# One PSUM tile per bank for the second mix, the attention product and the last part; attention in two blocks of work; an engine's own releases ahead of its pick

## The chip, the cores and the metric

The kernel runs on one core of a Trainium2 chip. The metric is device time in microseconds (us) of one execution; the median of three runs of the kernel before is 1122.73 us (1122.41 to 1123.28). A traced execution of it took 1125.21 us, with a span of 1123.4 us from its first to its last instruction; all rows below come from that execution.

## The reference

Attention with mixed heads (4 batches, 12 heads, 448 positions, 64 channels per head, all in 32-bit floats) is followed by two feed-forward layers over the 1792 rows that it makes:

```
scores = scale * matmul(q, k^T)                      # per batch and head
scores = einsum('bhij,hg->bgij', scores, w_pre)      # first mix, over heads
attn   = softmax(scores)
attn   = einsum('bhij,hg->bgij', attn, w_post)       # second mix, over heads
x      = matmul(attn, v)                             # attention product
h1 = ((x @ w1) * (x @ w2)) @ w3;   x1 = h1 @ w_out   # 768 -> 1024 -> 1024 -> 768
h2 = max(x1 @ m1, x1 @ m2, x1 @ m3); out = h2 @ m_out
```

The program fuses w3 and w_out into one matrix, and does every dense product with three passes over numbers that are split in a high and a low part.

## The kernel before

The program has two parts. The first is a list of pieces of work that `Plan` collects and orders; the second (`last_two`, from `seven`) is written in plain order and the framework schedules it.

In the first part the attention of all four batches runs, and beside it the fusing of weights (line 658) and the dense layers of batches 0 and 1 (line 753) fill TensorE (PE in the rows). A step of attention takes up to 20 query rows. Its PE pieces are: scores (line 379, tile `s`; in the beginning also `m` and `p`), the first mix (line 446, into `m`), and one step later the second mix (line 485, into `p`). ScalarE (ACT) and VectorE (DVE) reduce, take the exponential and evict. The evictions of the second mix go into the tile `a`: two copies by `copy` at line 280, one for each bank of `p`. After six steps (five or six in the last group of a batch) `attend` multiplies `a` by `v`: 36 matmuls over 128 rows (line 519) and then 12 over two halves of 64 rows for the last 64 keys (line 529), all into the two banks of `p`. Both banks are then evicted, for batch 0 into `X` (a copy by ACT and a subtraction by DVE each, line 541), otherwise into `xs`, and go to DRAM.

What stands in which order is set by `Plan.order`: it plays the pieces through with a cost for each (the second argument of `plan`), and an engine that comes free takes the ready piece with the smallest key; PE adds 0.5 (`STAY`) to the key of a piece in another mode. Modes are `q` (scores and both mixes, tiles of 64 rows), `a` (attention product) and `d` (dense and fusing, 128x128). In the event loop the end of a piece first makes the engine free (kind 0), then the engine picks, and only then are the pieces released that wait for the ended one on the same engine (kind 3); other engines' pieces follow after 0.12 (kind 1). So a dense piece that continues the one just ended is not yet on the list when PE picks.

All PSUM tiles come from one pool. `m`, `p` and `s` are tiles of two banks each (`banks`), and two single banks `w` serve the dense products: eight banks in all. The last part does the layers of batches 2 and 3 with seven products of half size instead of eight (`seven`); its accumulators p1 and p2 are the two banks of `m`, p6 and p5 those of `p`, p7 and p3 those of `s`, and p4 a `w` bank. ACT or DVE read each accumulator while PE goes on with the next (lines 997 to 1023), with weights that ACT and DVE split (lines 816 and 817).

Of the kernel before, what the change touches and what calls it, by code (L numbers as in the profile page):

```python
# [69 lines left out]
class Plan:  # L70
# [21 lines left out]
    def order(self):  # L92
# [25 lines left out]
        while True:  # L118
# [62 lines left out]
def attention_talking_heads_moe_kernel(  # L181
# [23 lines left out]
    stages = ctx.enter_context(ExitStack())  # L205
    pa = stages.enter_context(tc.tile_pool(name="pa", bufs=2))

    sdram = [dram.tile([S, H, S], F32, name=f"sdram_{b}") for b in range(B)]
# [4 lines left out]
    def bank():  # L213
        return ps.tile([P, 512], F32, tag="w", name="w", bufs=2)

    def banks(tag):
        return ps.tile([P, 2, 512], F32, tag=tag, name=tag, bufs=1)

# [112 lines left out]

    pm, pp, pz = (banks(x) for x in "mps")
    pw = [bank() for _ in range(2)]
# [30 lines left out]
    later = []  # L364

    def unit(b, r, u, slot, key, room="s"):

        whole = P * (r + 1) <= S
        parts = [(u, 0), (u, HB)] if whole else [(2 * u, 0), (2 * u + 1, 0)]
        pt = {"m": pm, "p": pp, "s": pz}[room]  # L370

# [3 lines left out]
        def multiply(_):  # L375
            for c, (pr, i) in enumerate(parts):
                for o in range(2):
                    sl = slice(o * D, (o + 1) * D)
                    nc.tensor.matmul(  # L379
                        pt[HB * c:HB * c + HB, o, :S], q[sl, pr, i:i + HB], kall[sl, pr], start=True, stop=True  # L380
                    )
# [3 lines left out]
        if r == 0 and b == 0:  # L385
            out, where = at[:, 2 * S * u:2 * S * (u + 1)], ("arow", u)
            out = out.rearrange("p (o j) -> p o j", o=2)
        else:
            n = turn("s", 2)
            out, where = st[n], ("st", n)  # L390

        def evict(e):
            if e == "ACT":
                nc.scalar.activation(out, pt[:, :, :S], AF.Copy, scale=D ** -0.5)
            else:
                nc.vector.tensor_scalar_mul(out, pt[:, :, :S], D ** -0.5)  # L396

        plan({"ACT": 0.95, "DVE": 1.12}, 0, key + 0.05, evict, bank_of, [where])
        if whole:
            x = 0 if r or b else P - 80  # L400
            reads = [where] if r or b else [("arow", y) for y in range(HP)]
            later.append(lambda: dma(
# [4 lines left out]
        else:  # L407
            for c, (pr, _) in enumerate(parts):
                dma("SP", key + 0.06, sdram[b][P * r:S, 2 * pr:2 * pr + 2], out[HB * c:HB * c + HB], 229e3,
                    [where], [("sd", b, r, pr)])  # L410

    def regroup(b, p, key):
# [5 lines left out]
        if b == 0 and i < FIRST:  # L418
            row = at
            for c in range(2):  # L420
                for u in range(2):
                    z = ROW[(i + GI * c + GB * u) // GB]
                    dma("POOL", key, x[HB * u:HB * u + MR, c], row[z:z + WAYS * (GB - 1) + 1:WAYS], 108e3,
                        [("arow", pr) for pr in range(HP)], [("x", n, u, c)])
        elif i + 2 * GI <= S:
# [43 lines left out]
    def post(b, p, e2, key):  # L469
        c0, i0, w = chunk(p)  # L470
        e_, kwr = es[e2], kwrs[e2]
        a = at[:, :JR * w].rearrange("p (r i) -> p r i", i=w)
        pt = pp[:, :, :JR * GI].rearrange("p c (r x) -> p c r x", x=GI)
        halves = [c for c in range(2) if blocks_of(p)[c][0]]

        def multiply(_):
            for u in range(2):
                for t in range(JF + 1):
                    for side in range(2):
                        j, g = (P * t + HB * side, 0) if t < JF else (S - HB, HP * side)  # L480
                        n = H if t < JF else HP
                        for c in halves:
                            m = blocks_of(p)[c][u]
                            sl = slice(HB * c, HB * c + MR)
                            nc.tensor.matmul(  # L485
                                pt[HB * side:HB * side + HB, c, H * t:H * t + n, u * GB:u * GB + m],
                                e_[sl, u, j:j + HB], kwr[sl, u, g:g + n, :m], start=True, stop=True,
# [4 lines left out]
        for c in halves:  # L492
            n = sum(blocks_of(p)[c])
            off = 2 * GI * p - i0 + GI * c
            whole = [("a", y, z) for y in range(CP) for z in range(2)]
            rows = [("arow", u) for u in range(HP)] if p == 0 and b == 0 else []
            plan({"ACT": 0.52, "DVE": 0.61}, 0, key + 0.03, lambda e, c=c, n=n, off=off: copy(
                e, a[:, :, off:off + n], pt[:, c, :, :n]),
                [("p", c)], (whole if p % CP == 0 and c == 0 else [("a", p % CP, c)]) + rows)
# [8 lines left out]
    def attend(b, p, key):  # L508
        _, i0, n = chunk(p)
        a = at[:, :JR * n].rearrange("p (r i) -> p r i", i=n)  # L510
        pt = pp[:, :, :3 * n].rearrange("p b (x i) -> p b x i", x=3)
        whole = [("a", y, z) for y in range(CP) for z in range(2)]

        def multiply(_):
            for pr in range(HP):
                for t in range(JF):
                    for o in range(2):
                        h = 2 * pr + o
                        nc.tensor.matmul(  # L519
                            pt[o * D:(o + 1) * D, pr // 3, pr % 3], vt[:, t, h * D:(h + 1) * D], a[:, t * H + h],  # L520
                            start=(pr % 3 == t == 0), stop=False,
                        )
            for pr in range(3):
                for x in range(2):
                    sl = slice(HB * x, HB * x + HB)
                    for o in range(2):
                        g = 2 * pr + o
                        h = HP * x + g
                        nc.tensor.matmul(  # L529
                            pt[o * D:(o + 1) * D, x, pr], vt[sl, JF, h * D:(h + 1) * D], a[sl, JF * H + g],  # L530
                            start=False, stop=(pr == 2),
                        )

        plan("PE", 4.35 * n / (CG * GI), key, multiply, whole + [("v", 0), ("v", 1, 0), ("v", 1, 1)],
             [("p", 0), ("p", 1)], mode="a")
        for x in range(2):
            if b == 0:
                sl, i = slice(3 * x, 3 * x + 3), slice(i0, i0 + n)
                plan("ACT", 0.5, key + 0.05, lambda _, sl=sl, i=i, x=x: nc.scalar.copy(
                    rows("X")[0][:, sl, i], pt[:, x]), [("p", x)], [("Xh", x, p // CP)] + [("Xh", y) for y in range(3)] * (p // CP == 0))  # L540
                plan("DVE", 0.58, key + 0.06, lambda _, sl=sl, i=i, x=x: nc.vector.tensor_sub(  # L541
                    rows("X")[1][:, sl, i], pt[:, x], rows("X")[0][:, sl, i].bitcast(F32)),
                    [("p", x), ("Xh", x, p // CP)],
# [4 lines left out]
            plan({"ACT": 0.5, "DVE": 0.58}, 0, key + 0.05, lambda e, t=t, x=x: copy(  # L548
                e, t, pp[:, x, :3 * n]), [("p", x)], [("xs", k)])
            dma("SP", key + 0.06, xdram[b][3 * x:3 * x + 3, :, i0:i0 + n].rearrange("x p i -> p x i"),  # L550
# [268 lines left out]
    def tail_parts(pool_users, at_):  # L819
# [294 lines left out]
    def attention_parts():  # L1114
# [19 lines left out]
        while later:  # L1134
            later.pop(0)()
        slots[0, 1] = load_q(0, 1, -5.6, after=[("arow", 2)])
        yield -1.0
        en = {}
        for s in range(LAST + LAG):
            if s == 1:  # L1140
                load_v(0, 3.0, [("arow", 5), ("sd", 0, 1, 1)])
            for d in (s + 2,):
# [112 lines left out]
```

## Time and profile before

| | us |
|---|---|
| median of three runs | 1122.73 |
| profiled execution | 1125.21 |
| its span | 1123.4 |
| PE busy (97% of the span) | 1085.8 |
| weight loads on PE (79%) | 882.1 |
| DVE busy (69%) | 774.6 |
| ACT busy (51%) | 568.2 |
| DMA moved 258.79 MB | 230 GB/s mean |

PE is busy in nearly the whole span, so the question at each place is not who waits for PE but what PE loses between pieces. A matmul's shown duration overlaps with the next one's; what a run of matmuls takes is read from the start of its first one to the start of the next run. The busy time of PE hides such losses, and a bracket at a row's end shows idle time only where nothing at all ran.

### The profile page before, as it was taken

The page shows a single profiled execution, that of the slowest core. Times are in us where ns is not written, and L with a number is a line of the kernel's source. Part 1 is how long each engine was busy: PE and PEld are TensorE (multiplying, and loading weights), DVE is VectorE, ACT ScalarE, POOL GpSimd, SP SyncE. Part 2 cuts the span into 40 slices and gives each one's busy share as a digit, 9 for nine tenths or more (in the row PEclk, how much of TensorE's full clock was granted, in tenths as well). Part 3 has the DMA queues.
Part 4 walks back from the last instruction along what each step waited for, and adds up shares of the span by engine and source line. Part 5 has one row for each costly group of instructions (what it writes and reads, how often), then busy time and mean ns, then how long its engine had stood idle before and what let it go on. Part 6 is the DMA issues. An engine that isn't in the chain of part 4 may idle for free.

```text
span 1123.4 us, 29327 instructions
## 1 busy us (share of the span) xinstructions
PE 1085.8 (97%) x12348; PEld 882.1 (79%) x12348; DVE 774.6 (69%) x1374; ACT 568.2 (51%) x1119; POOL 84.2 (7%) x159
## 2 busy tenths in 40 slices
PE   5799999999999999999999999999999999999998
PEld 1477787777777878777776888889788899888877
DVE  4775676678766877667667677783877753687874
ACT  4775566666466667555445454353433343233331
POOL 5310010000000100000111111110000000000000
PEclk8699999999999999999999999999999999999999
DMA  8989898989886989898998899877333321333333
GB/s 248 346 277 314 249 308 277 311 305 309 269 281 195 323 289 307 285 312 278 288 313 286 269 296 322 267 237 263 116 99 109 113 63 47 92 99 106 113 115 117
DMA packets 109365, 258.79 MB, mean 230 GB/s; under 512 B 21342, under 2 KB 61858, under 8 KB 109234
## 3 DMA queue, kind: packets, MB, share of 16 engines
q1 hardware_dynamic: 90290, 172.61, 47.8%
q0 software_dynamic: 16928, 80.64, 21.9%
q10 hardware_dynamic: 2016, 3.67, 0.9%
q8 instruction: 97, 1.59, 0.6%
q14 instruction: 34, 0.28, 0.1%
HBM read 173.84 MB, written 81.74 MB: 227 GB/s over the span
## 4 chain that ended last, share of the span: by engine, by line
PE 88%; DVE 6%; DMA 4%; ACT 1%; issue 1%; DVEq 0%; SPq 0%; ACTq 0%
PE w L753 31%; PE w L224 8%; PE p L485 7%; PE p L224 6%; PE m L446 6%; PE w L658 6%; PE s L379 6%; PE m L224 5%; PE s L224 5%; PE p L519 5%; PE p L529 1%; DMA wlo<-kept_m 1%; DMA sdram<-s 1%; DMA q<-in_qT 1%; DMA vlo<-sums_o 1%
## 5 line engine op out<-in xcount | busy, mean ns | idle before, releaser
L485 PEld LDWEIGHTS p<-kwr,e 60*64 60x64 f32 x5760 | 103.6, 137 | 46.0 <-issue 27.7
L450 DVE TENSOR_REDUCE nmax<-m 128x2 f32<-128x896 f32 (+1 forms) x92 | 100.1, 1088 | 43.6 <-PE m L446 43.2
L453 ACT ACTIVATE e<-m,nmax 128x448 f32<-128x448 f32 (+1 forms) x184 | 115.5, 637 | 16.1 <-DVE nmax L450 15.6
L485 PE MATMUL p<-kwr,e 60*64 60x60 f32 (+1 forms) x5760 | 103.6, 219 | 4.5 <-DVE xs L280 2.0
L280 ACT COPY a<-p 128x420 f32<-128x420 f32 (+1 forms) x114 | 56.0, 524 | 100.8 <-PE p L485 93.6
L446 PE MATMUL m<-x,kp 60*64 60x448 f32 x720 | 89.8, 558 | 1.0 <-ACT e L453 0.9
L379 PE MATMUL s<-kall,q 64*64 64x448 f32 x640 | 80.1, 571 | 8.9 <-DVE s L396 5.6
L753 PE MATMUL w<-yhi,whi 128*128 128x448 f32 x216 | 82.1, 380 | 0.0
L753 PE MATMUL w<-yhi,wlo 128*128 128x448 f32 x216 | 79.1, 366 | 0.1
L753 PE MATMUL w<-ylo,whi 128*128 128x448 f32 x216 | 78.9, 365 | 0.0
L753 PE MATMUL w<-xhi,whi 128*128 128x448 f32 x192 | 73.4, 382 | 0.0
L753 PE MATMUL w<-xlo,whi 128*128 128x448 f32 x192 | 70.2, 366 | 0.9 <-DVE xlo L541 0.9
L753 PE MATMUL w<-xhi,wlo 128*128 128x448 f32 x192 | 70.2, 366 | 0.0
L816 ACT CAST whi<-wlo 128x768 fp32r<-128x768 f32 x39 | 32.6, 835 | 70.0 <-DMA wlo<-sums_m 21.4
L753 PE MATMUL w<-hhi,whi 128*128 128x448 f32 x168 | 63.6, 379 | 0.0
L224 PE MATMUL p<-t,vhi 128*128 128x448 f32 x204 | 61.7, 373 | 0.7 <-DVE r L1003 0.4
L753 PE MATMUL w<-hhi,wlo 128*128 128x448 f32 x168 | 61.5, 366 | 0.5 <-DVE wlo L722 0.5
L722 DVE TENSOR_TENSOR wlo<-wlo,whi 128x256 fp32r<-128x256 f32 (+2 forms) x72 | 54.5, 774 | 10.1 <-ACT whi L721 10.0
L753 PE MATMUL w<-hlo,whi 128*128 128x448 f32 x168 | 61.4, 365 | 0.0
L519 PEld LDWEIGHTS p<-a,v 128*64 128x64 f32 x1152 | 55.3, 137 | 6.6 <-issue 3.7
L519 PE MATMUL p<-a,v 128*64 128x120 f32 (+1 forms) x1152 | 58.7, 261 | 1.2 <-ACT a L280 1.2
L816 ACT CAST vhi<-vlo 128x384 fp32r<-128x384 f32 (+1 forms) x39 | 25.9, 670 | 64.2 <-DMA vlo<-sums_m 26.2
(240 smaller groups left out, 2550.7 us busy)
## 6 DMA issues: line engine op xcount, KB each, us to landing
x<-sdram SPq DMA_DIRECT2D x170, 210.0 KB, 6.1
sdram<-s SPq DMA_DIRECT2D x66, 448.0 KB, 6.0
wraw<-in_wm POOLq DMA_DIRECT2D x18, 768.0 KB, 7.5
wlo<-kept_w SPq DMA_DIRECT2D x18, 512.0 KB, 4.0
wlo<-kept_m SPq DMA_DIRECT2D x23, 384.0 KB, 3.8
wraw<-in_w3T POOLq DMA_DIRECT2D x16, 512.0 KB, 6.7
kept_m<-wc SPq DMA_DIRECT2D x18, 384.0 KB, 6.0
wc<-kept_m POOLq DMA_DIRECT2D x18, 384.0 KB, 7.8
```

Source lines behind the costliest of these rows:

```text
L224: nc.tensor.matmul(out, w, r, start=(k == 0), stop=(k == 3 * n_k - 1))
L280: (nc.scalar.copy if e == "ACT" else ENG[e].tensor_copy)(out, src)
L379: nc.tensor.matmul(pt[HB * c:HB * c + HB, o, :S], q[sl, pr, i:i + HB], kall[sl, pr], start=True, stop=True)
L446: nc.tensor.matmul(pm[HB * c:HB * c + HB, u, :S], kp[sl], x[sl, c], start=True, stop=True)
L450: plan("DVE", 1.1, key + 0.01, lambda _: nc.vector.tensor_reduce(out=nmax[:r], in_=pm[:r, :, :S], axis=AX.X, op=ALU.max, negate=True), m_b ...
L453: plan("ACT", 0.85, key + 0.02, lambda _, u=u: nc.scalar.activation(e_[:r, u], pm[:r, u, :S], AF.Exp, bias=nmax[:r, u:u + 1], scale=1.0, a ...
L485: nc.tensor.matmul(pt[HB * side:HB * side + HB, c, H * t:H * t + n, u * GB:u * GB + m], e_[sl, u, j:j + HB], kwr[sl, u, g:g + n, :m], star ...
L519: nc.tensor.matmul(pt[o * D:(o + 1) * D, pr // 3, pr % 3], vt[:, t, h * D:(h + 1) * D], a[:, t * H + h], start=(pr % 3 == t == 0), stop=False,
L658: nc.tensor.matmul(pw[b][:, :FW], w, r, start=(k == 0 and i == 0), stop=(k == KH - 1 and i == 2))
L722: plan("DVE", 0.15 + 0.81 * w, key - 1.7, lambda _, hi=hi, lo=lo, t=t: nc.vector.tensor_sub(lo, t, hi.bitcast(F32)), list(reads) + mh, ml)
L753: nc.tensor.matmul(pw[w][:, :S], u, r, start=(k == 0 and i == 0), stop=(k == nk - 1 and i == 2))
L816: nc.scalar.copy(hi, t)
```

## The change

`Plan.order` gives the release of an engine's own followers the kind -1 in place of 3, so it comes ahead of the event that makes the engine free and lets it pick. `p` becomes two tiles of one bank each; scores that go through `p` are evicted in two pieces, one for each bank. `attend` is two pieces of work: the first does the last keys of both banks and then the 128-row products of bank 0, the second the 128-row products of bank 1; the last keys now stand first. The two-bank tiles live in a pool that is closed before the last part, which gets six tiles of one bank.

```diff
 class Plan:  # order()
-                    heapq.heappush(events, (now + took, 3, x, e))
+                    heapq.heappush(events, (now + took, -1, x, e))
...
-                    if same == (kind == 3):
+                    if same == (kind < 0):
...
-    pm, pp, pz = (banks(x) for x in "mps")
+    pm, pz = (pairs_of.tile([P, 2, 512], F32, tag=x, name=x) for x in "ms")
+    pp = [pairs_of.tile([P, 512], F32, tag=f"p{x}", name=f"p{x}") for x in range(2)]
...
 def unit:
+        if room == "p":
+            for o in range(2):
+                plan({"ACT": 0.52, "DVE": 0.6}, 0, key + 0.05, lambda e, o=o: evict(e, out[:, o], pt[o][:, :S]),
+                     bank_of[o:o + 1], where[o:o + 1])
...
 def attend:
-        plan("PE", 4.35 * n / (CG * GI), key, multiply, whole + [("v", 0), ("v", 1, 0), ("v", 1, 1)],
-             [("p", 0), ("p", 1)], mode="a")
         for x in range(2):
+
+            def multiply(_, x=x):
+                if x == 0:
+                    last_keys()
+                for pr in range(3):
+                    for t in range(JF):
+                        for o in range(2):
+                            h = 2 * (3 * x + pr) + o
+                            nc.tensor.matmul(
+                                pt[x][o * D:(o + 1) * D, pr], vt[:, t, h * D:(h + 1) * D], a[:, t * H + h],
+                                start=False, stop=(pr == 2 and t == JF - 1),
+                            )
+
+            f = n / (CG * GI)
+            plan("PE", (2.5, 1.9)[x] * f, key, multiply, whole + [("v", 0)] + [("v", 1, y) for y in range(2)] * (x == 0),
+                 [("p", y) for y in range(x, 2)], mode="a")
...
 def tail_parts, move:
             stages.close()
+            tail["banks"] = ctx.enter_context(tc.tile_pool(name="single", bufs=1, space=bass.MemoryType.PSUM))
...
 def seven:
-        p1, p2, p6, p5, p7, p3, p4 = [t[:, x, :S] for t in map(banks, "mps") for x in range(2)] + [bank()[:, :S]]
+        p1, p2, p6, p5, p7, p3 = (tail["banks"].tile([P, 512], F32, tag=x, name=x)[:, :S] for x in "126573")
+        p4 = bank()[:, :S]
```

The first place is PE around the fifth attention product (batch 1, first group), between a dense run and the next first mix. Before:

```order
L753 MATMUL w<-xhi,wlo 128x448
L519 MATMUL p<-a,v 64x120 x36
L529 MATMUL p<-a,v 64x120 x12
L446 MATMUL m<-x,kp 64x448 x4
L485 MATMUL p<-kwr,e 64x12x5 x12
```

and now (`p_189` and `p_190` are the two tiles of `p`; lines 529 and 543 are now the last keys and the 128-row products):

```order
L767 MATMUL w<-xhi,wlo 128x448
L529 MATMUL p_189<-a,v 64x120 x2
L529 MATMUL p_190<-a,v 64x120 x2
L529 MATMUL p_189<-a,v 64x120 x2
L529 MATMUL p_190<-a,v 64x120 x2
L529 MATMUL p_189<-a,v 64x120 x2
L529 MATMUL p_190<-a,v 64x120 x2
L543 MATMUL p_189<-a,v 64x120 x18
L543 MATMUL p_190<-a,v 64x120 x18
L454 MATMUL m<-x,kp 64x448 x4
L493 MATMUL p_189<-kwr,e 64x12x5
L493 MATMUL p_190<-kwr,e 64x12x5
```

The 64-row products moved ahead of the 128-row ones, and bank 0 is complete 18 matmuls before bank 1.

The second place is PE after the thirteenth attention product (batch 3, first group), where scores (line 379), dense work (753) and mixes alternate. Before:

```order
L379 MATMUL s<-kall,q 64x448 x4
L753 MATMUL w<-hhi,whi 128x448
L753 MATMUL w<-hlo,whi 128x448
L753 MATMUL w<-hhi,wlo 128x448
L753 MATMUL w<-hhi,whi 128x448
L753 MATMUL w<-hlo,whi 128x448
L753 MATMUL w<-hhi,wlo 128x448
L446 MATMUL m<-x,kp 64x448 x4
L485 MATMUL p<-kwr,e 64x12x5 x12
```

and now (the end of a second mix, then scores and the next first and second mix, lines 381, 454 and 493):

```order
L493 MATMUL p_189<-kwr,e 64x6x5
L493 MATMUL p_190<-kwr,e 64x6x5
L381 MATMUL s<-kall,q 64x448 x4
L454 MATMUL m<-x,kp 64x448 x4
L493 MATMUL p_189<-kwr,e 64x12x5
L493 MATMUL p_190<-kwr,e 64x12x5
```

The six dense matmuls no longer stand between the scores and the first mix. Over the whole first part PE has 108 unbroken dense runs before and 99 now, with the same 2112 dense matmuls.

The third place is PE in the last part, third call of `seven`, where p5 follows; a wait is named in brackets behind the instruction that has it. Before (`s` holds p7, the second `p` group is p5):

```order
L224 MATMUL s<-t_8923,whi 128x448 [waits DVE_49]
L224 MATMUL s<-t_8924,whi 128x448
L224 MATMUL s<-t_8923,wlo 128x448
L224 MATMUL s<-t_8923,whi 128x448
L224 MATMUL s<-t_8924,whi 128x448
L224 MATMUL p<-t_8927,vhi 128x448 [waits DVE_49]
L224 MATMUL p<-t_8928,vhi 128x448
```

and now (the tiles `6` and `5` are p6 and p5):

```order
L222 MATMUL 6_9348<-t_8935,vhi 128x448
L222 MATMUL 6_9348<-t_8936,vhi 128x448
L222 MATMUL 6_9348<-t_8935,vlo 128x448
L222 MATMUL 5_9349<-t_8931,vhi 128x448
L222 MATMUL 5_9349<-t_8932,vhi 128x448
```

The first matmul of p5 waited for a read by DVE of the tile that also holds p6, and five matmuls of p7 had been drawn ahead of it; now p5 follows p6 and waits for nothing. On DVE, 47 copies of line 280 carry a wait for ACT before, and 7 of the same line (now 278) in the changed program.

## Rows read from the trace of the kernel before

**Rows 1.** Windows by stage: stretch, length, busy time of each engine, granted clock, DMA share, GB/s.
```profile
0.00:62.00 62.00, 42.14 (x364) 22.96 (x364) 37.07 (x79) 36.85 (x76) 26.72 (x52) 0.75 0.92 305
206.00:767.00 561.00, 554.95 (x7917) 444.13 (x7920) 398.58 (x717) 311.00 (x639) 48.60 (x91) 1.00 0.87 285
791.50:1119.00 327.50, 323.13 (x1549) 286.93 (x1548) 224.83 (x360) 114.64 (x181) 0.00 (x0) 1.00 0.33 98
```

**Rows 2.** Chain that ended last, 240 to 268 us: start, length, what.
```profile
240.45 5.05 PE w L753 x24
...
253.18 2.63 PE w L753 x12
```

**Rows 3.** Timeline of PE, 240 to 268 us: start, duration, line, operation, count, idle before.
```profile
249.27 0.85 PE L529 MATMUL p<-a,v 64*64 64x120 f32 x24
249.94 0.93 PE L446 MATMUL m<-x,kp 60*64 60x448 f32 x8
251.26 1.13 PE L485 MATMUL p<-kwr,e 60*64 60x60 f32 x64 [0.40 <-DVE xs L280]
252.22 0.96 PE L379 MATMUL s<-kall,q 64*64 64x448 f32 x8
253.11 0.47 PE L753 MATMUL w<-xhi,whi 128*128 128x448 f32 x1
...
255.74 0.98 PE L446 MATMUL m<-x,kp 60*64 60x448 f32 x8
256.54 1.08 PE L485 MATMUL p<-kwr,e 60*64 60x60 f32 x64
...
265.18 0.98 PE L379 MATMUL s<-kall,q 64*64 64x448 f32 x8
265.98 0.93 PE L446 MATMUL m<-x,kp 60*64 60x448 f32 x8
266.73 1.08 PE L485 MATMUL p<-kwr,e 60*64 60x60 f32 x64
```

**Rows 4.** Timeline of all engines behind the fifth attention product.
```profile
250.18 0.46 ACT L280 COPY xs<-p 128x360 f32<-128x360 f32 x1 [3.12 <-PE p L529]
...
250.67 0.53 DVE L280 COPY xs<-p 128x360 f32<-128x360 f32 x1 [2.36 <-ACT xs L280]
251.12 1.08 DVE L450 TENSOR_REDUCE nmax<-m 128x2 f32<-128x896 f32 x1
```

**Rows 5.** Waits of PE, 62 to 791 us: total, times, longest.
```profile
PE p L485 <- DVE xs L280: 2.0, 5, 0.4
```

**Rows 6.** Timeline of PE where the dense layers of batch 0 begin.
```profile
201.24 0.47 PE L753 MATMUL w<-xhi,whi 128*128 128x448 f32 x1
202.64 0.47 PE L753 MATMUL w<-xlo,whi 128*128 128x448 f32 x1 [0.93 <-DVE xlo L541]
...
203.86 1.13 PE L485 MATMUL p<-kwr,e 60*64 60x60 f32 x64
```

**Rows 7.** Waits of the weight loads, 791.5 to 1119 us.
```profile
PEld p L224 <- DVE r L1003: 4.6, 14, 0.7
PEld m L224 <- ACT c L997: 2.7, 14, 0.2
```

**Rows 8.** Timeline of PE in one call of `seven`, around 836 and 840 us.
```profile
836.34 0.44 PE L224 MATMUL m<-xhi,whi 128*128 128x448 f32 x1
836.62 0.36 PE L224 MATMUL m<-xlo,whi 128*128 128x448 f32 x1
...
840.17 0.67 PE L224 MATMUL p<-t,vhi 128*128 128x448 f32 x2
840.68 0.36 PE L224 MATMUL p<-t,vlo 128*128 128x448 f32 x1
```

**Rows 9.** Timeline of PE before the thirteenth attention product.
```profile
615.63 0.42 PE L485 MATMUL p<-kwr,e 60*64 60x60 f32 x12 [1.28 <-issue]
617.29 0.94 PE L519 MATMUL p<-a,v 128*64 128x120 f32 x14 [1.24 <-ACT a L280]
```

More of the change, by code (lines that the diff above doesn't have):

```diff
@@ L206, in attention_talking_heads_moe_kernel @@
     pa = stages.enter_context(tc.tile_pool(name="pa", bufs=2))
+    pairs_of = stages.enter_context(tc.tile_pool(name="pairs", bufs=1, space=bass.MemoryType.PSUM))
     sdram = [dram.tile([S, H, S], F32, name=f"sdram_{b}") for b in range(B)]
@@ L214, in bank @@
         return ps.tile([P, 512], F32, tag="w", name="w", bufs=2)
-    def banks(tag):
-        return ps.tile([P, 2, 512], F32, tag=tag, name=tag, bufs=1)
     def products(out, pairs, n_k):
@@ L364, in attention_talking_heads_moe_kernel, with first_rows @@
     later = []
+    def first_rows(*units):
+        return [("arow", u, o) for u in units or range(HP) for o in range(2)]
     def unit(b, r, u, slot, key, room="s"):
@@ L369, in unit @@
         parts = [(u, 0), (u, HB)] if whole else [(2 * u, 0), (2 * u + 1, 0)]
-        pt = {"m": pm, "p": pp, "s": pz}[room]
+        pt = [pp[x] for x in range(2)] if room == "p" else [{"m": pm, "s": pz}[room][:, x] for x in range(2)]
         w = min(P, S - P * r)
@@ L379, in multiply @@
                     nc.tensor.matmul(
-                        pt[HB * c:HB * c + HB, o, :S], q[sl, pr, i:i + HB], kall[sl, pr], start=True, stop=True
+                        pt[o][HB * c:HB * c + HB, :S], q[sl, pr, i:i + HB], kall[sl, pr], start=True, stop=True
                     )
@@ L385, in unit @@
         if r == 0 and b == 0:
-            out, where = at[:, 2 * S * u:2 * S * (u + 1)], ("arow", u)
+            out, where = at[:, 2 * S * u:2 * S * (u + 1)], first_rows(u)
             out = out.rearrange("p (o j) -> p o j", o=2)
@@ L389, in unit, with evict @@
             n = turn("s", 2)
-            out, where = st[n], ("st", n)
-        def evict(e):
+            out, where = st[n], [("st", n)]
+        def evict(e, to, src):
             if e == "ACT":
-                nc.scalar.activation(out, pt[:, :, :S], AF.Copy, scale=D ** -0.5)
+                nc.scalar.activation(to, src, AF.Copy, scale=D ** -0.5)
             else:
-                nc.vector.tensor_scalar_mul(out, pt[:, :, :S], D ** -0.5)
-        plan({"ACT": 0.95, "DVE": 1.12}, 0, key + 0.05, evict, bank_of, [where])
+                nc.vector.tensor_scalar_mul(to, src, D ** -0.5)
+        if room == "p":
+            for o in range(2):
+                plan({"ACT": 0.52, "DVE": 0.6}, 0, key + 0.05, lambda e, o=o: evict(e, out[:, o], pt[o][:, :S]),
+                     bank_of[o:o + 1], where[o:o + 1])
+        else:
+            both = {"m": pm, "s": pz}[room][:, :, :S]
+            plan({"ACT": 0.95, "DVE": 1.12}, 0, key + 0.05, lambda e: evict(e, out, both), bank_of, where)
         if whole:
             x = 0 if r or b else P - 80
-            reads = [where] if r or b else [("arow", y) for y in range(HP)]
+            reads = where if r or b else first_rows()
             later.append(lambda: dma(
@@ L409, in unit @@
                 dma("SP", key + 0.06, sdram[b][P * r:S, 2 * pr:2 * pr + 2], out[HB * c:HB * c + HB], 229e3,
-                    [where], [("sd", b, r, pr)])
+                    where, [("sd", b, r, pr)])
     def regroup(b, p, key):
@@ L423, in regroup @@
                     dma("POOL", key, x[HB * u:HB * u + MR, c], row[z:z + WAYS * (GB - 1) + 1:WAYS], 108e3,
-                        [("arow", pr) for pr in range(HP)], [("x", n, u, c)])
+                        first_rows(), [("x", n, u, c)])
         elif i + 2 * GI <= S:
@@ L472, in post @@
         a = at[:, :JR * w].rearrange("p (r i) -> p r i", i=w)
-        pt = pp[:, :, :JR * GI].rearrange("p c (r x) -> p c r x", x=GI)
+        pt = [t[:, :JR * GI].rearrange("p (r x) -> p r x", x=GI) for t in pp]
         halves = [c for c in range(2) if blocks_of(p)[c][0]]
@@ L495, in post @@
             whole = [("a", y, z) for y in range(CP) for z in range(2)]
-            rows = [("arow", u) for u in range(HP)] if p == 0 and b == 0 else []
+            rows = first_rows() if p == 0 and b == 0 else []
             plan({"ACT": 0.52, "DVE": 0.61}, 0, key + 0.03, lambda e, c=c, n=n, off=off: copy(
-                e, a[:, :, off:off + n], pt[:, c, :, :n]),
+                e, a[:, :, off:off + n], pt[c][:, :, :n]),
                 [("p", c)], (whole if p % CP == 0 and c == 0 else [("a", p % CP, c)]) + rows)
@@ L510, in attend, with last_keys @@
         a = at[:, :JR * n].rearrange("p (r i) -> p r i", i=n)
-        pt = pp[:, :, :3 * n].rearrange("p b (x i) -> p b x i", x=3)
+        pt = [t[:, :3 * n].rearrange("p (x i) -> p x i", x=3) for t in pp]
         whole = [("a", y, z) for y in range(CP) for z in range(2)]
[L514 to L522, printed above, removed]
+        def last_keys():
             for pr in range(3):
@@ L539, in attend @@
                 plan("ACT", 0.5, key + 0.05, lambda _, sl=sl, i=i, x=x: nc.scalar.copy(
-                    rows("X")[0][:, sl, i], pt[:, x]), [("p", x)], [("Xh", x, p // CP)] + [("Xh", y) for y in range(3)] * (p // CP == 0))
+                    rows("X")[0][:, sl, i], pt[x]), [("p", x)], [("Xh", x, p // CP)] + [("Xh", y) for y in range(3)] * (p // CP == 0))
                 plan("DVE", 0.58, key + 0.06, lambda _, sl=sl, i=i, x=x: nc.vector.tensor_sub(
-                    rows("X")[1][:, sl, i], pt[:, x], rows("X")[0][:, sl, i].bitcast(F32)),
+                    rows("X")[1][:, sl, i], pt[x], rows("X")[0][:, sl, i].bitcast(F32)),
                     [("p", x), ("Xh", x, p // CP)],
@@ L1135, in attention_parts @@
             later.pop(0)()
-        slots[0, 1] = load_q(0, 1, -5.6, after=[("arow", 2)])
+        slots[0, 1] = load_q(0, 1, -5.6, after=first_rows(2))
         yield -1.0
```

10 lines of the change are left out of this document (5 added, 5 removed).

## The prediction

> **What bounds the kernel now.** I read the busy shares first, then the windows by stage, then the timeline of PE at the borders between its kinds of work, then the lists of waits, and last the two orders. By the windows PE is busy in 554.95 of 561 us of the long middle and 323.13 of 327.5 us of the last part, at a granted clock of 1.00 [rows 1]. So the kernel is PE's, and nothing that only spares DVE or ACT counts. What can change is what PE loses between pieces. The first 62 us are another regime: PE is busy for 42.14 us at a mean granted clock of 0.75 (so partly at the lower of its two levels, 1.2 GHz instead of 2.4), with transfers at a share of 0.92. The order of PE, ACT and DVE is nearly the same there in both programs, so I give that stretch no term.
>
> The sum is made against the profiled execution (1125.21 us; span 1123.4 and 1.8 around it). That is 2.5 us above the median of 1122.73, and I take the sum off the median.
>
> **Fewer borders between kinds of work.** 24 dense matmuls take 5.05 us and 12 take 2.63 [rows 2], so twelve more cost 2.42 and every unbroken run has 2.63 - 2.42 = 0.21 us on top of its matmuls. In the 64-row pieces, scores that are followed by dense work take 0.89 us from start to start (252.22 to 253.11), and scores between dense work and a mix 0.80; a mix behind dense work takes 0.80 (255.74 to 256.54), one behind scores 0.75 (265.98 to 266.73) [rows 3]. So a 64-row block pays 0.05 for coming after dense work, and 0.89 - 0.75 = 0.14 for going back to it. The two orders differ by 9 dense runs (108 to 99), 5 returns from 64-row pieces to dense work (102 to 97) and 10 entries from dense work into them (94 to 84). That is 9 x 0.21 + 5 x 0.14 + 10 x 0.05 = 1.89 + 0.70 + 0.50 = 3.1 us gained. Most of it is the second place of the orders: a dense run of six no longer slips between scores and mix, because the follower of a PE piece is on the list when PE picks.
>
> **The last keys first.** Before, dense work is followed by the 128-row products, then the 64-row ones, then the mix. Now it is 64 rows, 128 rows, 64 rows: at each of the 16 attention products one entry and one return more, less 4 returns, since 6 products led straight from the 64-row part to dense work and now 2 lead there from the 128-row part. No row shows the border from 64-row products to the 128-row attention ones. If it costs what the return to dense work does, it is 16 x (0.14 + 0.05) - 4 x 0.14 = 2.5 us lost. If it costs nothing, as the border in the other direction seems to (the 24 passes of the 64-row part keep 0.67 us, 249.27 to 249.94 [rows 3]), it is 0. I take 2.4, near the upper end, because the kind of border is the same.
>
> The Trainium skill speaks against this part: in TensorEngine Tiling (Array Packing), section Key Properties, it says that a change of tiling mode drains the engine, whichever way it goes. By that rule each of the 16 added borders costs, and the sum has the 2.5; by the 0.67 us alone it would have 0 and the forecast would be 2.4 us lower. The 0.14 at the return to dense work agrees with the rule, the border into the 64-row part does not show it.
>
> **The wait behind the attention product.** The mix behind the fifth product takes 1.32 us to the second mix (249.94 to 251.26) where 0.75 is its own time. The second mix waits for the copies of both banks, and these ran one behind the other: ACT from 250.18 for 0.46 us, DVE from 250.67 for 0.53, held by ACT [rows 3, 4]. There are five such waits [rows 5]: 5 x (1.32 - 0.75) = 2.9 us. Now bank 0 is complete 18 matmuls earlier and its copy lies beside the rest of the product. Bank 1 has a tile and a reader of its own, and its copy needs 0.06 (250.12 to 250.18) + 0.53 us, which the first mix (0.75) covers. All 2.9 us go, if the engine is free (below).
>
> **The start of the dense layers.** Their first six matmuls took 2.62 us (201.24 to 203.86) for 0.21 + 6 x 0.2017 = 1.42, because PE waited for the low part of `X` [rows 6]. The first piece of six needs only the half that comes from bank 0, whose copy and subtraction now run beside the second block. I count 1.2 us gained; the bounds are 0 and 1.2.
>
> **The last part.** A call of `seven` waits in two places: p2 for ACT's read of p1, and p5 for DVE's read of p6, 14 times each [rows 7]. PE's matmuls follow each other at 0.202 us; here one step takes 0.28 (836.34 to 836.62) and two take 0.51 (840.17 to 840.68) [rows 8], so 0.08 + 0.10 us are lost. 14 x 0.18 = 2.5 us is what the starts show; 4.6 + 2.7 = 7.3 us, the idle time of the weight loads, is the upper bound, since loads run ahead of matmuls. With a tile for each bank both waits are gone from the order (its third place). I take 3.5, nearer to the starts. The lower bound is 0: DVE is busy 224.83 of 327.5 us with adds and weight splits, and PE could meet the next split sooner.
>
> **Copies of the second mix.** The DVE copies held by ACT fall from 47 to 7. Mostly a dense run follows and nobody waits for them. Before the thirteenth attention product PE stands still for 1.24 us until ACT's copy is done [rows 9]; the other bank's copy on DVE had to end first, about 0.5 us like those in rows 4. I count 0.5 us gained. The 1.28 us without a named cause in the row before it may fall elsewhere in another order; that is 0 in the sum and 1.3 either way in the range. The two score tiles of `p` that are now evicted in halves are 2 of 6 at the very start, spread over two engines: 0.
>
> **Sum.** -3.1 + 2.4 - 2.9 - 1.2 - 3.5 - 0.5 = -8.8 us. 1122.73 - 8.8 = 1113.9 us.
>
> **Rivals.**
> - *A late reader of bank 1 (slower).* The copy of bank 1 stands in a queue on DVE or ACT. If each of the 16 has a reduction of 1.08 us ahead of it that starts as the product ends, the second mix waits 1.08 + 0.53 + 0.06 - 0.75 = 0.92 us: 14.7 us in all. Without the wait's own 2.9 the sum is -5.9, so the time is 1122.73 - 5.9 + 14.7 = 1131.5 us. It decides from a mean wait of 0.37 us on. For it: DVE is busy 398.58 of 561 us [rows 1], and the reduction in rows 4 starts just behind the copy. Against it: both copies in rows 4 started within 0.06 us of what they waited for, and the planner lays the second mix only where it expects the copies done. The Trainium skill (PSUM — Partial Sum Buffer, section Engine vs sequencer instructions) says that these queues are strict first in, first out, so nothing would pass the reduction; the trace agrees, in that no row here shows a DVE or ACT instruction out of its order.
> - *The transfers bind.* Their share is 0.87 in the middle [rows 1]. Then what PE gains there comes back as waits for loads and only the last part (share 0.33) keeps its 3.5: 1119.2 us. Against it: PE stood still for only 6 of 561 us.
> - *No change.* The added borders eat the ones saved, the second mix finds another late copy for the five waits, and in the last part p2 or p5 waits for a weight split in place of the read: 1122 us.
>
> **How the numbers follow.** I give the forecast 0.68, the transfers 0.13, no change 0.10, the late reader 0.09. Predicted time 1114 us. The range goes from 1107 (the borders of the attention product at 0, -2.4, and the last part at its 7.3, -3.8) to 1121.5, which takes in the transfers and part of no change. A measurement can tell about 0.2% (2.2 us) from no change, so faster is below 1120.5: 0.66 of the forecast, 0.10 of the transfers and 0.02 of no change make 0.78; slower is the late reader and a little of no change, 0.10; 0.12 is left for the same.
>
> **What would show it.** In the trace after: second mixes behind an attention product with 0.75 to 0.80 us from the first mix's start, and the copy of bank 0 running beside the 128-row products of bank 1; the first six dense matmuls in about 1.42 us; no wait of PE for the reads of p1 and p6, and calls of `seven` that take about 0.2 us less; scores, first and second mix in one block with 0.34 us for each dense run less. The step from the 64-row passes to the 128-row ones shows what the new border costs. I am wrong if copies of bank 1 start later than 0.4 us after the product, if the dense stretches have new waits for transfers or splits, or if the first 62 us, with their low clock, come out otherwise by more than 2 us.

## The result and the profile after

Beside each other on one chip, the kernel before took 1123.01 us (1122.41 to 1123.45) and the changed one 1108.73 us (1104.27 to 1110.84): a ratio of 0.9865, 95% interval [0.9835, 0.9896]. It is faster, by more than the forecast's 8.8 us. Measured twice more on other occasions, it came to 0.9803 [0.9773, 0.9833] and 0.9815 [0.9787, 0.9842], at medians of 1102.97 and 1104.98 us. Those two lie below the low end of the range, 1107 us.

The traced execution of the changed kernel took 1110.84 us with a span of 1109.1. Its windows over the stretches of [rows 1], same columns:

```profile
0.00:62.00 62.00, 42.42 (x361) 22.43 (x362) 35.86 (x78) 36.93 (x77) 26.38 (x51) 0.72 0.91 299
206.00:767.00 561.00, 556.89 (x7947) 444.99 (x7946) 405.06 (x720) 306.43 (x641) 48.87 (x91) 1.00 0.88 286
791.50:1119.00 327.50, 313.65 (x1521) 284.68 (x1519) 221.31 (x354) 108.80 (x174) 0.00 (x0) 1.00 0.32 96
```

The first 62 us are nearly what they were, and the middle gets more PE work done in the same 561 us. The last window ends behind the program's end now. The last part went from 791.5 to 1118.9 us (327.4) before and goes from 785.7 to 1104.8 (319.1), each time from the start of its first matmul to the start of its last one. So of 14.3 us between the two traces, the first part gave 5.8 and the last part 8.3. Such a split holds for these two executions alone: in the run of the last part's tiles alone (below) the first part, with its order of before, ended at 794.6 us in place of 791.5, so some 3 us between two traces can be spread.

The timeline around the fifth attention product, the place of [rows 3, 4]:

```profile
244.53 0.85 PE L529 MATMUL p<-a,v 64*64 64x120 f32 x24
245.31 3.91 PE L543 MATMUL p<-a,v 128*64 128x120 f32 x72
...
247.42 0.53 DVE L278 COPY xs<-p 128x360 f32<-128x360 f32 x1 [2.32 <-PE p L543]
...
249.15 0.98 PE L454 MATMUL m<-x,kp 60*64 60x448 f32 x8
249.26 0.46 ACT L278 COPY xs<-p 128x360 f32<-128x360 f32 x1 [2.17 <-PE p L543]
249.95 1.08 PE L493 MATMUL p<-kwr,e 60*64 60x60 f32 x64
```

Bank 0 is copied from 247.42 on, beside the 128-row products of bank 1, and bank 1 at 249.26, beside the mix. The second mix follows the first one's start by 0.80 us instead of 1.32. All ten second mixes that come this way show 0.80. The 24 passes of the last keys now take 0.78 us instead of 0.67.

PE where the dense layers begin [rows 6]: six matmuls in 1.42 us.

```profile
201.13 0.47 PE L767 MATMUL w<-xhi,whi 128*128 128x448 f32 x1
201.44 0.37 PE L767 MATMUL w<-xlo,whi 128*128 128x448 f32 x1
...
202.55 0.67 PE L493 MATMUL p<-kwr,e 60*64 60x60 f32 x32
```

Not all went well. PE's waits from 62 to 785 us (total, times, longest) have a new line at their head, where [rows 5] stood, and the timeline shows its larger piece:

```profile
PE m L454 <- ACT e L461: 3.0, 2, 2.1
```

```profile
611.85 1.13 PE L493 MATMUL p<-kwr,e 60*64 60x60 f32 x64
615.07 0.98 PE L454 MATMUL m<-x,kp 60*64 60x448 f32 x8 [2.10 <-ACT e L461]
```

A first mix waits there for ACT's exponential to give `m` free. At the same time of its trace, right before the thirteenth product, the kernel before had lost 1.28 and 1.24 us [rows 9], so about as much is lost there as before. It is no fixed loss: the same line has 2.3 and 0.9 us in the two later traces of the changed kernel.

In the last part the waits of the weight loads, the view of [rows 7], are almost gone. This is the whole list after:

```profile
PEld 5_9128 L222 <- ACT t L874: 0.3, 1, 0.3
PEld 5_9128 L222 <- DVE t L875: 0.2, 1, 0.2
```

Below the two lines of [rows 7], the list of before went on with these (lines 816 and 817 are the weight splits):

```profile
PEld w L224 <- ACT vhi L816: 1.8, 1, 1.8
PEld w L224 <- DVE vlo L817: 1.3, 2, 0.7
PEld s L224 <- DVE r L1014: 1.3, 5, 0.4
PEld p L224 <- ACT vhi L816: 1.2, 1, 1.2
PEld p L224 <- DVE ylo L817: 0.7, 1, 0.7
PEld p L224 <- DVE vlo L817: 0.7, 1, 0.7
PEld p L224 <- ACT t L859: 0.6, 1, 0.6
PEld m L224 <- DVE p0lo L817: 0.5, 1, 0.5
```

With [rows 7] that is 15.4 us of idle weight loads. I had counted two of the three lines on reads of a shared tile (the third, L1014 with 1.3 us, is DVE's read of p7 that p3 waits for); the 6.2 us of waits for splits went as well. PE's matmuls themselves lost less. Most of them start 0.20 to 0.21 us behind the one before; the steps of 0.225 us and over held 10.9 us beyond that in the kernel before and 0.3 us in the changed one. By the wait of the weight load beside each such step, about 4.2 of the 10.9 us stand at the two lines of [rows 7], 0.7 at the third and 5.6 at the splits.

### The profile page after: what moved, and what is told of

Read it like the earlier page. It is cut to its first block, busy times and chain, and to the rows that moved or that the text cites. A ratio compares the mean times of both kernels' runs of the same rounds, so it can differ in the third digit from the quotient of the medians.

```text
span 1109.1 us, 29315 instructions
## 1 busy us (share of the span) xinstructions
PE 1080.0 (97%) x12348; PEld 883.0 (80%) x12348; DVE 781.9 (71%) x1379; ACT 557.8 (50%) x1116; POOL 84.6 (8%) x159
## 4 chain that ended last, share of the span: by engine, by line
PE 93%; DMA 3%; DVE 2%; ACT 1%; issue 0%; SPq 0%; ACTq 0%; DVEq 0%
PE w L767 32%; PE w L222 9%; PE p L493 7%; PE m L454 7%; PE w L672 6%; PE s L381 6%; PE p L543 5%; DMA sdram<-s 2%; PE p L529 1%; DMA q<-in_qT 1%; DMA kall<-in_kT 0%; DVE v L594 0%; PE m L381 0%; PE p L381 0%; DVE s L398 0%
## 5 line engine op out<-in xcount | busy, mean ns | idle before, releaser
L493 PEld LDWEIGHTS p<-kwr,e 60*64 60x64 f32 x5760 | 106.5, 137 | 40.4 <-issue 31.5
L461 ACT ACTIVATE e<-m,nmax 128x448 f32<-128x448 f32 (+1 forms) x184 | 115.5, 637 | 15.7 <-DVE nmax L458 15.2
L454 PE MATMUL m<-x,kp 60*64 60x448 f32 x720 | 92.1, 572 | 3.0 <-ACT e L461 3.0
L398 DVE TENSOR_SCALAR s<-s 128x896 f32<-128x896 f32 x53 | 57.7, 1089 | 8.9 <-PE s L381 4.7
L594 DVE SCALAR_TENSOR_TENSOR wc<-wc,wraw 128x768 uint32<-128x768 uint32 (+1 forms) x56 | 49.0, 876 | 8.2 <-ACT wc L591 6.0
```

The lines of the kernel that those rows point to most:

```text
L398: nc.vector.tensor_scalar_mul(to, src, D ** -0.5)
L454: nc.tensor.matmul(pm[HB * c:HB * c + HB, u, :S], kp[sl], x[sl, c], start=True, stop=True)
L461: plan("ACT", 0.85, key + 0.02, lambda _, u=u: nc.scalar.activation(e_[:r, u], pm[:r, u, :S], AF.Exp, bias=nmax[:r, u:u + 1], scale=1.0, a ...
L493: nc.tensor.matmul(pt[c][HB * side:HB * side + HB, H * t:H * t + n, u * GB:u * GB + m], e_[sl, u, j:j + HB], kwr[sl, u, g:g + n, :m], star ...
```

## The experiments

My theory after the first comparison: the tiles of the last part gave the larger share, the release change most of the rest, and the last keys first cost some of it back. The rival, that the parts simply add up as in the prediction's sum, is in the expectations.

**The release change alone**, on the kernel before:

```diff
-                    heapq.heappush(events, (now + took, 3, x, e))
+                    heapq.heappush(events, (now + took, -1, x, e))
-                    if same == (kind == 3):
+                    if same == (kind < 0):
```

> The kernel before with the release change alone (an engine's own followers are released ahead of its pick); tiles and attention as before. Theory: it makes 99 dense runs of 108 and leaves three attention products of five with the first and second mix right behind them. 3.1 us for the borders and 2 x 0.57 us for the waits: about 1118.8 us, with the six first dense matmuls still at 2.6 us and the last part still at 327 us. Rival (the other stalls of the first part move with any new order and are as large as this): anywhere from 1117 to 1125 us, with stalls of over 1 us at new places.

1117.90 us, ratio 0.9926 [0.9899, 0.9954]. The first part ended 7.1 us earlier (784.4), the last one stayed at 328.8 us. Of the five waits behind the attention product two are left, one of 0.4 us for ACT's copy behind the twelfth product is new, and the wait for the low part of `X` is half as long. PE's waits from 200 to 783 us in this kernel:

```profile
PE w L753 <- DVE wlo L722: 1.6, 3, 0.9
PE p L485 <- DVE xs L280: 0.6, 2, 0.4
...
PE w L753 <- DVE xlo L541: 0.4, 1, 0.4
PE p L485 <- ACT xs L280: 0.4, 1, 0.4
```

So this edit gave more than the 3.1 us of its borders: it took waits that the prediction had given to the blocks.

**The tiles of the last part alone**, on the kernel before:

```diff
-        p1, p2, p6, p5, p7, p3, p4 = [t[:, x, :S] for t in map(banks, "mps") for x in range(2)] + [bank()[:, :S]]
+        p1, p2, p6, p5, p7, p3 = (tail["banks"].tile([P, 512], F32, tag=x, name=x)[:, :S] for x in "126573")
+        p4 = bank()[:, :S]
```

> The kernel before with six tiles of one bank in the last part alone; the order of the first part is unchanged. Theory: the waits for a read of the other bank were all that held PE in the last part, the stalls at its beginning (about 2.9 us) and at 1078 to 1095 us (about 3.2 us) included, because PE now has the matmuls of p1 and p2 to do while operands come; the last part takes 319 to 320 us instead of 327.4: about 1114.7 us. Rival: only the two waits in each call of seven go, and the stalls at its beginning and end went in the changed kernel because its first part ended earlier: the last part then takes about 323 us, 1118.5 us.

1114.06 us, ratio 0.9891 [0.9869, 0.9912]; the last part took 313.9 us instead of 327.4. The waits of its weight loads, all of them:

```profile
PEld 2_11439 L222 <- ACT p0hi L814: 0.3, 1, 0.3
PEld w L222 <- ACT hhi L814: 0.2, 1, 0.2
PEld 6_9124 L222 <- ACT t L858: 0.2, 1, 0.2
```

This edit alone takes 14.7 of the 15.4 us, those behind the weight splits too. The split work is the same, but the order of PE is not: in the traces the 1548 matmuls of the last part stood in 209 runs on one tile, with 187 weight loads that carry a wait, and now stand in 157 runs with 153 such loads. Whether the order or the missing waits let PE meet finished splits was not tried apart.

**The last keys last**: the changed kernel with `attend` as one piece on the one-bank tiles, the 64-row products at its end.

```diff
+        def multiply(_):
+            for pr in range(HP):
+                for t in range(JF):
...
+            last_keys()
-        for x in range(2):
-            plan("PE", (2.5, 1.9)[x] * f, key, multiply, whole + [("v", 0)] + ...
+        plan("PE", 4.35 * n / (CG * GI), key, multiply, whole + [("v", 0), ("v", 1, 0), ("v", 1, 1)],
+             [("p", 0), ("p", 1)], mode="a")
```

> The changed kernel with the attention product as one piece of work and the last keys at its end again, on two tiles of one bank. Theory: the copies of the two banks run side by side and need no more than 0.6 us, which the first mix covers, so no wait comes back; the added borders go (16 x 0.16 us = 2.5 us) and the first six dense matmuls wait again for X (1.2 us): 1.3 us less than the changed kernel, about 1107.4 us. Rival (bank 0 must be complete early): waits of about 0.5 us come back behind the products, 1109 to 1110 us.

1103.78 us, ratio 0.9802 [0.9777, 0.9826], in another set of runs than the first comparison, which leaves this open; hence the comparison further below.

**No release change**, the rest of the change kept:

```diff
-                    heapq.heappush(events, (now + took, -1, x, e))
+                    heapq.heappush(events, (now + took, 3, x, e))
-                    if same == (kind < 0):
+                    if same == (kind == 3):
```

> The changed kernel without the release change: tiles and two blocks of the attention product stay, and own followers are again released after the pick. In its order the second block of the product is never on the list when the first ends, so other work stands between the two at all 16 products, and there are 113 dense runs. Theory: 14 more dense runs (2.9 us), 16 more borders inside the products at 0.1 to 0.3 us (3 us) and six more entries (0.3 us): about 6 us more than the changed kernel, 1114.5 us; the last part stays at 319 to 320 us. Rival (borders cost nothing where other work fills PE's waits): within 2 us of the changed kernel.

1108.74 us, ratio 0.9850 [0.9828, 0.9871]: near the first comparison, so it looked like the rival. The timeline suggests why the loss is small. Twelve dense matmuls stand between the two blocks of the fifth product; behind the second block, the first row here, PE goes on with scores, mixes and dense work. No second mix meets a late copy:

```profile
245.70 2.07 PE L543 MATMUL p<-a,v 128*64 128x120 f32 x36
247.69 0.98 PE L381 MATMUL s<-kall,q 64*64 64x448 f32 x8
248.50 0.93 PE L454 MATMUL m<-x,kp 60*64 60x448 f32 x8
249.25 1.08 PE L493 MATMUL p<-kwr,e 60*64 60x60 f32 x64
250.26 0.47 PE L767 MATMUL w<-xhi,whi 128*128 128x448 f32 x1
```

**The changed kernel again**, with three of its relatives on one chip (no edit):

> The changed kernel itself, again, for its spread and for a second trace. In the first trace the matmuls of the last part followed each other at 0.206 us, in that of the last part's tiles alone at 0.202 us. Theory: the step has two values and a gapless stretch keeps the one it fell into, so the last part takes about 314 us at the low one and 319 to 320 us at the high one, whatever the order of the work; the executions of this one program then spread over 5 to 7 us (1104 to 1111) and this trace may show either. Rival: the slower step belongs to the program, and the last part takes 319 us again with a spread below 3 us.

1102.97 us (1100.74 to 1107.82), ratio 0.9803 [0.9773, 0.9833]: a spread of 7.1 us, as the theory had it. The last part of its trace took 317.9 us, with both steps in it (windows further below).

**The last keys last again** (no new edit):

> The changed kernel with the attention product as one piece and the last keys last, beside the changed kernel on one chip. Theory (16 added borders at 0.16 us): 2.5 us below the changed kernel, about 1104 to 1105 us. Rival (the borders are free in time, and the 0.6% between the two ratios so far is the chip's or the step's): within 1 us of the changed kernel.

1102.18 us, ratio 0.9805 [0.9775, 0.9835]: within 1 us of the changed kernel, as the rival had it. In the traces its first part ended at 782.0 us against 783.9, in the direction of the theory, but the times don't separate the two.

**The last keys last without the release change**: the edits of those two together.

> As the run before in this call, without the release change: the order of pieces of the kernel before, on one-bank tiles. Theory (the release change saves 9 dense runs and 10 entries, 3.1 us, where attention is one piece; run alone it gave 8 us on another chip, waits included): 3 to 5 us above its neighbour, 1107 to 1109 us. Rival (what the one-bank tiles gain and what the release change gains is the same idle time): within 1 us of it.

1112.92 us, ratio 0.9879 [0.9850, 0.9907]: 10.7 us above its neighbour, more than twice what the theory said, though its trace is only 5.6 us longer in the first part (787.6 us). Where the rest of the 10.7 us lies is not shown. Two of PE's waits from 200 to 783 us in it, the low part of `X` (0.4 us in the neighbour) and a copy that the neighbour doesn't wait for:

```profile
PE w L764 <- DVE xlo L552: 0.9, 1, 0.9
...
PE p L539 <- DVE a L278: 0.8, 1, 0.8
```

**The old tiles in the last part** of the changed kernel:

```diff
-        p1, p2, p6, p5, p7, p3 = (tail["banks"].tile([P, 512], F32, tag=x, name=x)[:, :S] for x in "126573")
-        p4 = bank()[:, :S]
+        both = (tail["banks"].tile([P, 2, 512], F32, tag=x, name=x) for x in "mps")
+        p1, p2, p6, p5, p7, p3, p4 = [t[:, x, :S] for t in both for x in range(2)] + [bank()[:, :S]]
```

> The changed kernel with the two-bank tiles back in the last part alone. Theory (the tiles of the last part take away some 11 us of stalls, whatever stands ahead): 11 to 13 us above the changed kernel, 1118 to 1120 us, the last part 327 to 329 us long with 11 to 13 us of stalls. Rival (the 8.3 us by which the last part shortened in the first two traces are all there is, since stalls and the slow step exclude each other): 6 to 8 us above it, 1114 us.

1118.18 us, ratio 0.9928 [0.9900, 0.9956], 15.2 us above the changed kernel; the last part took 330.4 us. The waits for reads of the other bank are back, so it was the tiles that took them away and not the new pool of PSUM tiles, which this run has too:

```profile
PEld p L222 <- DVE r L1019: 2.8, 10, 0.4
PEld m L222 <- ACT c L1013: 2.7, 14, 0.3
```

The loss is more than expected, and two windows show one reason (columns as in [rows 1]):

```profile
795.00:800.00 5.00, 5.00 (x16) 4.45 (x15) 1.80 (x4) 0.00 (x0) 0.00 (x0) 0.54 0.00 0
800.00:805.00 5.00, 5.00 (x26) 4.32 (x25) 3.44 (x6) 1.78 (x3) 0.00 (x0) 1.00 0.41 124
```

PE never stood still in these first 5 us, yet did 16 matmuls instead of 26: after a series of stalls from 789 to 794 us the granted clock fell to 0.54, most of the time the lower level of 1.2 GHz. The run of the release change alone shows the like: 18 matmuls from 795 to 800 us at 0.66.

**The changed kernel a third time**, with the last three (no edit):

> The changed kernel beside the three others of this call, 1103 to 1107 us. If the two values of the matmul step are a thing of the execution and not of the program, the last part of this trace takes anything between 314 and 320 us, and its change from 0.202 to 0.207 us, or back, stands elsewhere than at 890 us.

1104.98 us (1100.68 to 1110.84), ratio 0.9815 [0.9787, 0.9842]. Two windows of the last part, of the second trace and of this one, same program:

```profile
800.00:860.00 60.00, 60.00 (x298) 55.60 (x297) 46.13 (x74) 20.96 (x35) 0.00 (x0) 1.00 0.36 106
920.00:980.00 60.00, 60.00 (x293) 54.49 (x291) 34.55 (x54) 21.70 (x35) 0.00 (x0) 1.00 0.25 73
```

```profile
800.00:860.00 60.00, 60.00 (x292) 54.50 (x291) 45.08 (x72) 19.75 (x33) 0.00 (x0) 1.00 0.35 106
920.00:980.00 60.00, 60.00 (x292) 54.51 (x291) 33.32 (x51) 20.81 (x33) 0.00 (x0) 1.00 0.25 76
```

Without an idle moment, 60 us hold 298 matmuls or 292 (those that reach in from outside are counted too), at the same granted clock; from start to start that is 0.2027 us for each in the one and 0.2067 in the other. One execution changes from the one to the other between 880 and 920 us, the other is slow in both. So the step belongs to the execution and not to the program. Over 1548 matmuls the difference is 6.2 us, where each set of times of the changed kernel spreads by 6.6 to 10.2 us. That the step makes this spread is not shown, since the fastest executions were not traced.

**Six times the borders** in the attention product of the changed kernel:

```diff
-                if x == 0:
-                    last_keys()
                 for pr in range(3):
+                    last_keys(x, pr)
                     for t in range(JF):
```

> The changed kernel with the last keys of each pair of heads right ahead of that pair's 128-row products: 96 borders from 64-row products to 128-row ones instead of 16, and 79 back inside the product. Theory (a border into 128-row products costs 0.11 us as in the trace of the changed kernel, one into 64-row pieces 0.05): 80 x 0.16 = 12.8 us above the changed kernel, and each product 0.8 us longer. Rival (the 0.11 us belong to the border to the evicted or first-read bank, not to the change of rows; or the borders fall into time that PE has to spare): less than 3 us above it.

1134.37 us, ratio 1.0084 [1.0067, 1.0101]: 29.4 us above the changed kernel, more than twice the theory. For 80 added pairs of borders that is 0.37 us a pair. PE at the fifth product:

```profile
251.37 0.42 PE L527 MATMUL p<-a,v 64*64 64x120 f32 x4
251.72 0.84 PE L540 MATMUL p<-a,v 128*64 128x120 f32 x12
252.49 0.42 PE L527 MATMUL p<-a,v 64*64 64x120 f32 x4
252.84 0.84 PE L540 MATMUL p<-a,v 128*64 128x120 f32 x12
```

These rows count every matmul of the orders twice. Twelve products take 0.77 us where 72 in a row take 3.84, and four key passes 0.35 where 24 take 0.78. By the two lengths a product costs (3.84 - 0.77) / 60 = 0.051 and its border to 64 rows 0.15 us; a key pass costs (0.78 - 0.35) / 20 = 0.0215 and its border to 128 rows 0.26 us. Both directions cost, and nothing hides them. Their sum, 0.41, is a little above the 0.37; the products at the end of a batch are shorter.

**No release change again** (no new edit):

> The changed kernel without the release change, now on one chip with it. Theory (9 dense runs and 10 entries more, as in the sum of the prediction, and the start of the dense layers late by 0.5 us): 3 to 4 us above the changed kernel. Rival (with the attention product in two blocks other work fills the waits, so the release change is worth nothing): within 1 us.

1108.47 us, ratio 0.9855 [0.9835, 0.9875]: 3.5 us above the changed kernel beside it, with a first part that ended at 786.5 us against 783.3. The rival falls, and with it the earlier reading, which had compared ratios of different sets of runs; but narrowly, as the two sets overlap (1107.52 to 1113.56 and 1100.68 to 1110.84). The theory's number came out, its sum did not: I took the 9 dense runs and 10 entries from the prediction, where attention is one piece. This order has 113 dense runs against 99, 14 more, and other work between the two blocks at all 16 products, for which the expectation of the first such run had about 6 us. So what the 3.5 us are made of is not shown.

**The release change and the tiles of the last part, nothing else**: the first two diffs together.

> The kernel before with the release change and the six tiles of one bank in the last part, and nothing else: p stays one tile of two banks, the attention product one piece with its last keys last. Theory (the one-bank p tiles and the two blocks take away two waits of 0.57 us behind the product and give 2.5 us back at the added borders): 0 to 1.5 us below the changed kernel. Rival (the blocks gain what the prediction counted, 2.9 us and the 1.2 us at the start of the dense layers, beyond the borders): 1.5 to 3 us above it.

1105.46 us (1104.15 to 1106.36), ratio 0.9816 [0.9800, 0.9832]: 0.5 us from the changed kernel. Two of the old waits and the new one for ACT's copy are still there; here is the one behind the sixth product:

```profile
295.61 0.84 PE L527 MATMUL p<-a,v 64*64 64x120 f32 x24
296.28 0.93 PE L444 MATMUL m<-x,kp 60*64 60x448 f32 x8
297.60 1.13 PE L483 MATMUL p<-kwr,e 60*64 60x60 f32 x64 [0.39 <-DVE xs L278]
```

The first part ended at 784.5 us; in the three traces of the changed kernel it ended at 785.7, 783.9 and 783.3. The one-bank tiles of `p` and the two blocks gain nothing that can be measured on top of these two edits. Without the release change they do gain: in the first set of experiments, on one chip, the changed kernel without it took 1108.74 us (1108.44 to 1111.62) and the kernel before with the last part's tiles alone 1114.06 (1113.75 to 1114.94), and these two differ by the one-bank tiles of `p` and the blocks alone. That is 5.3 us. So the release change and the blocks are largely after the same lost time, and whichever is made first gets it.

## Why the prediction was right, and where it was not

The direction and the mechanisms held; several sizes did not.

- *The last part* is the step that failed: "I take 3.5, nearer to the starts", with 7.3 as the upper bound. Measured, 8.3 us in the first trace and 13.5 us alone. The bound was made from two of the ten lines of that list. At their places PE lost about 4.2 us, near the 3.5; what I put at nothing were the splits, about 5.6 us, and the third read, 0.7. I took the waits for weight splits for a limit of ACT and DVE and even gave "DVE is busy" as the reason for a lower bound of 0. The tiles alone removed them, with the same splits; by which way stays open. The difference between 8.3 and 13.5 is the matmul step. Outside the stalls the last part ran at a mean of 0.2046 us before, 0.2061 in the changed kernel and 0.2027 with the tiles alone. At an equal step both traces give the same, 10.5 to 10.7 us of stalls gone.
- *Fewer borders*, -3.1: too small for the edit, and as the price of these borders neither confirmed nor refuted. The changed kernel without it took 3.5 us more, but with other counts of borders than the sum's. With the attention product in one piece it gave 7.1 us of the first part between two traces, because it also took three of the five waits (1.7 us, less 0.4 for the new one) and 0.5 us at the dense layers' start. The other 2.2 us beyond the 3.1 were not assigned to a place, and are within the spread between traces.
- *The waits behind the product*, -2.9, and *the start of the dense layers*, -1.2: each place came out as forecast (0.80 us, 1.42 us). But these gains were not the blocks' own: with the release change made, two waits of 0.57 us, the new one of 0.4 and 0.7 us at the start (200.34 to 202.46 us in the run of two edits) were left for them, 2.3 us. *The copies*, -0.5: the wait named is gone, and 2.1 us ahead of a first mix stand close by in the first trace, so no net gain is shown.
- *The last keys first*, +2.4: by 0.11 (0.67 to 0.78) and the 0.05 of the entry it is 16 x 0.16 = 2.5 us. By these counts it eats what was left of the blocks' gain; the last keys last, measured beside the changed kernel, came out 0.8 us below it, within the spread. The Trainium skill (TensorEngine Tiling (Array Packing), section Key Properties) has the drain at either change of mode; the run with six times the borders agrees, with 0.37 us for a pair.
- *The rivals.* No second mix waited for a late copy of bank 1, so the late reader is out. The transfers did not bind: their share rose to 0.88 and the middle still gained. "No change" named a wait for a weight split in place of the read; the opposite happened.
- *The range* held the first comparison (1108.73 us), and not the two later ones, because it took its lower end from the 7.3 us. That the first one lies in it is in part luck: in the traced execution the slower step took 5.3 us of the last part, against 3.0 before.

## What to carry to other kernels

When two accumulators share a tile, price the change to separate tiles by all waits of the stage, not only by those that name the tile's readers, and bound it by the sum of the list. When several edits aim at the same wait, price each one without the others before adding. Separate tiles and followers that are on the list at the pick were cheap edits; together they gave all of this gain. The rearranged attention product added nothing to them that could be measured, though without the second of them it was worth 5.3 us, together with the one-bank tiles of `p`.

## What the runs showed of the hardware

- A gapless run of 128x448 matmuls keeps one of two steps, 0.2027 or 0.2067 us, for hundreds of matmuls at a granted clock of 1.00. What sets it stays open; in the last part here it is worth up to 6.2 us from one execution to the next.
- Stalls can cost twice: behind those at the start of the last part the granted clock was 0.54 over 5 us with the old tiles in the changed kernel (10 matmuls fewer) and 0.66 with the release change alone; in the traced execution of the kernel before it stayed at 1.00 at that place.
- A pair of borders between 64-row and 128-row products costs 0.37 us in the run with six times the borders, on a path where PE is always busy.
- The Trainium skill (Perfetto Trace Analysis, section Matmuls) has independent groups rotate through PSUM banks so that one is read out while the next is filled. Before, the banks did rotate, but two shared a tile and the reads still held PE: 8.6 of the 15.4 us of idle weight loads name such a read, and with a tile for each bank all that is left is 0.7 us.
